# A head pair's order on five engines in hand, with its array visits, query casts and weight pieces moved, in a chunk-select attention with a routed expert layer

## The chip, the cores and the metric

The kernel runs on one core of one Trainium2 chip. The metric is the device time of one execution in microseconds (us), lower is better. The core has TensorE (PE; PEld is its weight load), VectorE (DVE), ScalarE (ACT), GpSimd (POOL), SyncE (SP), and 16 DMA engines that SP, ACT and POOL feed.

## The reference

Two stages follow each other. Attention: 4 batches, 8 heads, 768 positions, head size 64. Keys are cut into chunks of 32; for each query an upper bound of its score with any key of a chunk is formed, and the query attends, causally, to the 6 chunks of the highest bound:

```python
ub = np.sum(np.maximum(q[:, :, :, None, :] * k_min[:, :, None, :, :],
                       q[:, :, :, None, :] * k_max[:, :, None, :, :]), axis=-1)
ub = np.where(causal, ub, -1e9)
top_chunks = np.argsort(ub, axis=-1)[..., -top_k:]
...
attn = softmax of q @ k.T / 8 over the kept positions        # in words
x = (attn @ v) as 3072 tokens x 512
```

Then every token goes to the one expert of 8 with the highest logit `x @ w_gate`, and its output row is `gate * (relu(x @ w1[e]) @ w2[e])`, with w1 512x1024 and w2 1024x512 for each expert and gate the softmax probability of that expert.

## The kernel before, in words

**Tiling.** Attention runs over 16 head pairs `i` (4 in a batch; `hp = i % 4`). The two heads of a pair lie side by side in partitions. Scores are formed transposed (keys in partitions, queries in columns, queries in two halves of 384) in seven units `u`, 0 and 1 for the first query half, 2 to 6 for the second. A unit is one score tile in PSUM (two buffers, `ps_s`), an exp on ACT (L303), a causal `affine_select` on POOL for diagonal blocks (L307), a product with V on PE that collects in `po` (L320, `attend`), and an addition on DVE of the exponentials to an accumulator that gives the softmax sum (L332). Units 1 and 6 hold two key blocks, of 256 and 128 columns, each with an exp and an addition of its own. The chunk choice enters the scores as extra rows of the two operands: rows 64 and up of `KTE` name the chunk of a key, those of `QSB` hold which chunks a query does not take.

**Steps of a pair besides its units.** For pair `i+2`: K's two halves transposed on PE, their chunk maxima and minima on DVE (L207, L208) and scaled copies on ACT (L209, L210), in `k_half`; Q's halves transposed, copied on DVE and ACT (L224 to L227), and the query operand of head 0 cast on POOL (L226, kept back in `late` until a `flush`); sums and differences of maxima and minima (`kse`, L233 and L234). For pair `i+1`: the bound product (`ub`, L241), its choice of chunks on DVE (`select`, L249 to L262), and the mask's transposes (`mask`, L269) with two copies on ACT. For pair `i-1`: a product `ud` (L348, L353) that yields the softmax sums and the gate logits, its transposes `lgp` (L361), and the output rows `x0`, `x1` (L386, L388). Once a batch is complete its tokens are routed: `logits` (L398 to L422), `rank` (L432 to L448) and six scatters to HBM (L454). All small PSUM tiles share one pool of three buffers, `ps_m`.

**Array shapes.** The trace shows PE's matmuls as 128*128, 128*64 (L320, L241, L269) and 128*32 (`ud`).

**Order.** PE, POOL and SP follow the order of the code (`manual_schedule`); DVE and ACT are ordered by a scheduler, except in the first pair and from pair 15 on. The driver runs each pair in four groups g = 0 to 3: scores of units 2 and 3, then 4 and 5, then 6, then units 0 and 1 of pair `i+1`; in each, other steps stand between the scores and the attend products:

```python
groups = [(0, 1), (2, 3), (4, 5), (6,)]
spread = ((), (0,), (2, 4), (1,), (3, 5), (), (), ())
        wq += [4 * i + g for g in ((0, 1, 2) if i in (1, 3, 4, 8, 12) else (1, 2))]
```

`wq` sets in which group each of 32 weight pieces (512 KB, `load_w`, L169, issued by POOL) is fetched; pair 15 has none. `load` fetches K and Q of pair `i+3` in group 3 and V of pair `i+1` in group 0, issued by SP. `spread` sets where a batch's scatters go.

**The second stage.** A table of 28 tiles of 128 tokens of one expert is built in two parts (`table`, the first in pairs 13 and 14, L477 on). A tile's rows are gathered from HBM (L554, POOL), transposed by DMA (`x_in`, L566, SP), multiplied by w1 (`up`, L601), passed through ReLU (L604, ACT), transposed by DMA again (`hT`, L605, SP), multiplied by w2 (`down`, L612), scaled by the gate and scattered to the output (L620). Gathers 0 to 3 are issued at the start of pair 15, 4 to 7 in its third group; they use four buffers, freed by `x_in` and `meta`. `up` and `down` address the weights through a register.

Of the kernel before, what the change touches and what calls it, by code (L numbers as in the profile page):

```python
# [24 lines left out]
def kernel(  # L25
# [10 lines left out]
    nc = tc.nc  # L36
# [63 lines left out]
    KS = [buf.tile([128, 64], FP32, name=f"KS{i}") for i in range(2)]  # L100
    KD = [buf.tile([128, 64], FP32, name=f"KD{i}") for i in range(2)]
# [6 lines left out]
    def consts_first():  # L108
# [12 lines left out]
        nc.gpsimd.memset(KS[0][:], 0.0)  # L121
        nc.gpsimd.memset(KD[0][:], 0.0)
# [15 lines left out]
    def consts_last():  # L138
        nc.gpsimd.memset(KS[1][:], 0.0)
        nc.gpsimd.memset(KD[1][:], 0.0)  # L140
# [7 lines left out]
        nc.sync.dma_start(out=wgb[64:128, :, E:2 * E], in_=wg_v[64:128])  # L148
        iota(rev8[:], [[-1, E]], base=E)
# [11 lines left out]
    def load_w(s_):  # L161
# [7 lines left out]
        nc.gpsimd.dma_start(out=dst, in_=src.rearrange("(c p) f -> p c f", p=128))  # L169
# [24 lines left out]
    def prep_steps(i):  # L194
        s = st[i]
        kte, qsb, ks, kd = KTE[i % 2], QSB[i % 2], KS[i % 2], KD[i % 2]
        kmx = {}

        def k_half(hf):
# [3 lines left out]
            pt = ps_m.tile([128, 384], FP32, tag="m")  # L203
            for t in range(3):
                nc.tensor.transpose(pt[:, ts(t, 128)], s["k"][:, 3 * hf + t], ident_f[:])
            pk = pt[:].rearrange("p (c w) -> p c w", w=CH)
            nc.vector.tensor_reduce(s["kmx"][:, ts(hf, 12)], pk, AX.X, ALU.max)  # L207
            nc.vector.tensor_reduce(s["kmn"][:, ts(hf, 12)], pk, AX.X, ALU.min)  # L208
            nc.scalar.activation(kte[0:64, 0, ts(hf, 384)], pt[0:64, :], AF.Copy, bias=0.0, scale=0.125)  # L209
            nc.scalar.activation(kte[0:64, 1, ts(hf, 384)], pt[64:128, :], AF.Copy, bias=0.0, scale=0.125)  # L210

        def q_t(hf):
            pt = ps_m.tile([128, 384], FP32, tag="m")
            for t in range(3):
                nc.tensor.transpose(pt[:, ts(t, 128)], s["q"][:, 3 * hf + t], ident_f[:])
            s[f"qp{hf}"] = pt

        def q_e(hf):
            pt = s[f"qp{hf}"]
            if hf == 0:  # L220
                s["qT"] = work.tile([128, 2, 384], FP32, tag="qT", name="qT")
                s["qA"] = work.tile([128, 2, 384], FP32, tag="qA", name="qA")
            qT, qA = s["qT"], s["qA"]
            nc.vector.tensor_copy(out=qT[:, hf], in_=pt[:])  # L224
            nc.scalar.activation(qA[:, hf], pt[:], AF.Abs)
            late.append(lambda: nc.gpsimd.tensor_copy(out=qsb[0:64, 0, ts(hf, 384)], in_=qT[0:64, hf]))  # L226
            nc.scalar.activation(qsb[0:64, 1, ts(hf, 384)], pt[64:128, :], AF.Copy)  # L227

        def kse():
            for hd in range(2):  # L230
                r = slice(64 * hd, 64 * hd + 64)
                c = slice(32 * hd, 32 * hd + NCH)
                nc.vector.tensor_tensor(ks[r, c], s["kmx"][r, :], s["kmn"][r, :], ALU.add)  # L233
                nc.vector.tensor_tensor(kd[r, c], s["kmx"][r, :], s["kmn"][r, :], ALU.subtract)  # L234

        def ub():
            pu = ps_m.tile([128, 384], FP32, tag="m")
            for w_, nm in ((ks, "qT"), (kd, "qA")):
                x_ = s[nm][:].rearrange("p a c -> p (a c)")
                for h in range(2):  # L240
                    nc.tensor.matmul(pu[64 * h:64 * h + 64, 0:320], lhsT=w_[:], rhs=x_[:, ds(128 + 320 * h, 320)],  # L241
                                     start=(nm == "qT"), stop=(nm == "qA"), skip_group_check=True)
            s["ubT"] = work.tile([128, 384], FP32, tag="ud", name="ubT")
            nc.scalar.activation(s["ubT"][:, 0:320], pu[:, 0:320], AF.Copy)

        def select():
            pt = ps_m.tile([128, 3, 2, 2, 32], FP32, tag="m")
            for t in range(3):
                nc.tensor.transpose(pt[:, t], s["ubT"][:, ds(c0s[t], 128)], ident_f[:])  # L249
            ubm = work.tile([128, 3, 2, 2, NCH], FP32, tag="ubm")  # L250
# [623 lines left out]
```

## Time and profile before

| | |
|---|---|
| median of 3 runs | 359.88 us (358.68 to 360.48) |
| the profiled execution | 360.64 us |
| its span in the trace, granted clock | 358.6 us, 0.992 |
| busy share of the span: PE, DVE, ACT, POOL | 91, 66, 64, 50% |
| attention, up to the first `up` | 0 to 243.1 us |
| from one `lgp` (L361) to the next, pairs with no routing | 13.66 us |
| the same, pairs 5 and 9, which rank a batch | 15.51 us |
| weight pieces, issue to landing, median | 6.0 us |
| up and down of one token tile on PE, late in the second stage | 3.45 us |

A line of a timeline gives start and length in us, engine, line, operation, what is written and read, the number of instructions joined in it, and in brackets the idle time ahead of it with what ended it. A start is to be read against its neighbours: `L361` at 128.29 and at 141.95 delimit a pair. Busy shares are of the whole span; In the last third DVE is nearly idle and ACT half idle, so in the first two thirds they are far busier than the table says.

### The profile page before, as it was taken

How to read it: one execution, taken by the hardware profiler on the slowest of the kernel's cores; microseconds unless marked ns; L12 is line 12 of the kernel's file. 1: busy time of each engine (PE TensorE's matmuls, PEld its weight loads, DVE VectorE, ACT ScalarE, POOL GpSimd, SP SyncE). 2: the span in 40 equal slices, each digit the busy share in tenths (PEclk: the TensorE clock that was granted, in tenths of full speed). 3: DMA queues.
4: the chain of work that ended last, by engine and by line, in shares of the span. 5: the costliest groups of instructions: out<-in, count | busy, mean ns of one | idle time of the engine just before them, and what ended most of it. 6: DMA issues, size and time to landing. Idle time of an engine off the chain costs nothing. (4 is left out here: it accounts for less than half of the span.)

```text
span 358.6 us, 7585 instructions
## 1 busy us (share of the span) xinstructions
PE 326.9 (91%) x2312; PEld 171.5 (48%) x2312; DVE 235.0 (66%) x815; ACT 231.2 (64%) x398; POOL 180.4 (50%) x296
## 2 busy tenths in 40 slices
PE   6679999999899999999999988998799999999990
PEld 5535455455455465554554545443344344444430
DVE  5799889889999898999988999846460000000000
ACT  2497797797687897867977967642344444445440
POOL 3075425445474453466534547575577665653331
PEclk9999999999999999999999999999999999999996
DMA  8619998999957999937989973476999999998851
GB/s 153 112 26 194 210 220 139 215 167 215 207 127 151 182 176 195 202 100 178 200 134 212 187 148 113 73 135 116 165 211 233 221 237 197 203 186 201 157 126 48
DMA packets 138215, 59.83 MB, mean 167 GB/s; under 512 B 122811, under 2 KB 131005, under 8 KB 138176
## 3 DMA queue, kind: packets, MB, share of 16 engines
q1 hardware_dynamic: 119072, 29.52, 45.4%
q0 software_dynamic: 17536, 29.42, 42.0%
q10 hardware_dynamic: 1568, 0.39, 0.6%
q8 instruction: 21, 0.34, 0.4%
q14 instruction: 18, 0.15, 0.2%
HBM read 56.14 MB, written 10.51 MB: 186 GB/s over the span
## 5 line engine op out<-in xcount | busy, mean ns | idle before, releaser
L332 DVE TENSOR_TENSOR Pa<-Pa,Pr 128x768 f32<-128x768 f32 (+2 forms) x112 | 81.6, 729 | 1.1
L307 POOL TENSOR_SCALAR_AFFINE_SELECT Pr<-Pr 128x256 f32<-128x256 f32 x80 | 33.5, 437 | 67.3 <-ACT Pr L303 66.1
L303 ACT ACTIVATE Pr<-ps 128x768 f32<-128x768 f32 (+2 forms) x112 | 65.0, 630 | 3.2 <-PE ps L298 2.9
L612 PE MATMUL py<-w_all,hT 128*128 x224 | 52.7, 379 | 2.7 <-DMA hT<-h__3653 1.9
L298 PE MATMUL ps<-QSB,KTE 128*128 128x384 bf16 (+2 forms) x288 | 50.4, 292 | 1.2 <-DVE QSB L711 0.2
L620 POOL DMA_INDIRECT out_dram<-y,ti_all x28 | 27.8, 993 | 30.2 <-ACT y L619 26.3
L298 PEld LDWEIGHTS <-KTE 128*128 128x128 bf16 x288 | 24.1, 97 | 27.3 <-issue 21.2
L612 PEld LDWEIGHTS <-hT 128*128 128x128 bf16 x224 | 21.8, 98 | 29.5 <-DMA hT<-h__3653 2.3
L619 ACT ACTIVATE y<-py,gt_all 128x512 f32<-128x512 f32 x27 | 18.6, 687 | 20.8 <-PE py L612 18.4
L454 POOL DMA_INDIRECT xs_dram<-xrow,sli x24 | 26.9, 1121 | 7.7 <-issue 5.0
L356 ACT ACTIVATE ud<-pu 128x384 f32<-128x384 f32 x16 | 7.9, 492 | 32.8 <-PE pu L353 30.7
L303 ACT ACTIVATE Pa<-ps 128x768 f32<-128x768 f32 x32 | 26.0, 812 | 3.8 <-PE ps L298 3.2
L601 PE MATMUL ph<-w_all,KTE 128*128 x120 | 28.4, 379 | 0.0
L169 POOL DMA_DIRECT2D w_all<-in_moe_w_dram x32 | 24.3, 760 | 0.0
L307 POOL TENSOR_SCALAR_AFFINE_SELECT Pa<-Pa 128x256 f32<-128x256 f32 x16 | 6.4, 398 | 35.3 <-ACT Pa L303 35.3
L601 PE MATMUL ph<-w_all,QSB 128*128 x96 | 22.7, 379 | 0.3 <-issue 0.3
L575 DVE TENSOR_TENSOR ti_all<-xgqA,inv_i 128x1 int32<-128x1 int32 x9 | 1.4, 159 | 29.6 <-DMA xgqA<-xs_dram,grow 29.6
L554 POOL DMA_INDIRECT xgqA<-xs_dram,grow x14 | 14.6, 1046 | 10.2 <-issue 3.3
L554 POOL DMA_INDIRECT xgqT<-xs_dram,grow x14 | 14.5, 1033 | 8.7 <-DVE gt_all L577 4.9
L325 DVE COPY ot<-po 128x384 f32<-128x384 f32 x32 | 17.7, 553 | 1.6 <-PE po L320 0.9
L575 DVE TENSOR_TENSOR ti_all<-xgqT,inv_i 128x1 int32<-128x1 int32 x8 | 1.3, 159 | 26.5 <-DMA xgqT<-xs_dram,grow 26.5
L226 POOL CAST QSB<-qT 64x384 bf16<-64x384 f32 x30 | 16.3, 551 | 4.1 <-DVE qT L224 2.8
(311 smaller groups left out, 665.0 us busy)
## 6 DMA issues: line engine op xcount, KB each, us to landing
w_all<-in_moe_w_dram POOLq DMA_DIRECT2D x32, 512.0 KB, 6.0
out_dram<-y,ti_all POOLq DMA_INDIRECT x28, 3.6
t__122<-in_k_dram SPq DMA_DIRECT2D x2, 192.0 KB, 3.5
t__125<-in_q_dram ACTq DMA_DIRECT2D x2, 192.0 KB, 4.0
t__128<-in_v_dram SPq DMA_DIRECT2D x2, 192.0 KB
t__196<-in_k_dram SPq DMA_DIRECT2D x2, 192.0 KB, 3.1
t__206<-in_q_dram SPq DMA_DIRECT2D x2, 192.0 KB, 3.8
t__209<-in_v_dram SPq DMA_DIRECT2D x2, 192.0 KB
```

Source lines behind the costliest of these rows:

```text
L169: nc.gpsimd.dma_start(out=dst, in_=src.rearrange("(c p) f -> p c f", p=128))
L298: nc.tensor.matmul(pv[:, hd, :], lhsT=kte[:, hd, ts(kb, 128)], rhs=qsb[:, hd, ds(qb * 384 + 384 - w, w)], start=True, stop=True, skip_grou ...
L303: nc.scalar.activation(P[:, :, ds(c0, w)], pv, AF.Exp)
L307: nc.gpsimd.affine_select(out=pd, in_=pd, pattern=[[0, 2], [1, 128]], compare_op=ALU.is_ge, fill=0.0, base=0, channel_multiplier=-1)
L325: nc.vector.tensor_copy(out=ot[:], in_=po[:])
L332: nc.vector.tensor_tensor(acc[:, :, 384 - w:384], acc[:, :, 384 - w:384], P[:, :, ds(c0, w)], ALU.add)
L454: d = nc.gpsimd.indirect_dma_start(out=xs_dram[:], out_offset=bass.IndirectOffsetOnAxis(ap=sli[:, u:u + 1], axis=0), in_=bst[b][f"xrow{u % ...
L554: d = nc.gpsimd.indirect_dma_start(out=xg_bufs[j % XB].bitcast(I32), out_offset=None, in_=xs_dram[:], in_offset=bass.IndirectOffsetOnAxis( ...
L601: nc.tensor.matmul(ph[:, fh, :], lhsT=xT[:, c, :], rhs=w_all[:, ds(wo + (c * F + fh * 512), 512)], start=(c == 0), stop=(c == NDC - 1), sk ...
L612: nc.tensor.matmul(py[:], lhsT=hT[:, c, :], rhs=w_all[:, ds(wo + (W1W + c * DM), DM)], start=(c == 0), stop=(c == NFC - 1))
L619: nc.scalar.activation(y[:], py[:], AF.Copy, bias=0.0, scale=fs[j]["gt"])
L620: d = nc.gpsimd.indirect_dma_start(out=out[:], out_offset=bass.IndirectOffsetOnAxis(ap=fs[j]["ti"], axis=0), in_=y[:], in_offset=None, bou ...
```

## The change

- `KS` and `KD` become one tile `KSD`; `kse` has three DVE operations for four, one of them a product with a constant block mask `bm`.
- The constants of routing and table leave `consts_last` for `consts_route`, called in pair 2, group 2.
- w2's pieces are loaded with `(p c) f` rows, a partition's four rows of w2 adjacent in HBM; ReLU writes h in the matching order, reading PSUM in strides of four.
- All steps are cut into a PE part (`_mm`), a DVE part (`_v`) and an ACT part (`_a`), and DVE and ACT follow the order of the code throughout.
- A unit's columns lie at the same place in each head's half of the score tile, so units 1 and 6 have one exp. Unit 6 is scored in halves of 64 keys (`split`), eight matmuls for four.
- The driver has another order: unit 6's scores move from group 2 to the end of group 1, `ud` behind them, and the mask behind `ud`. K's first half goes from group 2 to group 1, its ACT copies ahead of its DVE reductions. The additions of units 5 and 6 go to the next pair's group 0. The query casts on POOL (`flush(late)`) go from group 0 to group 1, ahead of unit 6's affine selects.
- Logits of a batch go from group 3 of the pair with hp = 0 to group 0 of the next, and are whole there; rank, exp and gates follow in its group 1, the scatters in other groups.
- Weight pieces go by `npiece`: one at the start of group 0, the others in group 1; pair 15 has three, issued after gathers 0 to 3 and ahead of gathers 4 to 7.

The diff, cut to its core:

```diff
-        nc.gpsimd.dma_start(out=dst, in_=src.rearrange("(c p) f -> p c f", p=128))
+        nc.gpsimd.dma_start(out=dst, in_=src.rearrange("(c p) f -> p c f" if n < 2 else "(p c) f -> p c f", p=128))
...
+        def kse():
+            kt2 = work.tile([128, 2, NCH], FP32, tag="top8", name="kt2")
+            nc.vector.tensor_tensor(kt2[:, 0], s["kmx"][:], s["kmn"][:], ALU.add)
+            nc.vector.tensor_tensor(kt2[:, 1], s["kmx"][:], s["kmn"][:], ALU.subtract)
+            nc.vector.tensor_tensor(ksd[:, :, :, 0:NCH], kt2[:].unsqueeze(2).to_broadcast([128, 2, 2, NCH]),
+                                    bm[:].unsqueeze(1).to_broadcast([128, 2, 2, NCH]), ALU.mult)
...
+        n = 64 if split else 128
+        for kb, w, c0 in parts:
+            for hd in range(2):
+                for h in range(128 // n):
+                    nc.tensor.matmul(ps[ds(h * n, n), hd, ds(c0, w)], lhsT=kte[:, hd, ds(kb * 128 + h * n, n)],
+                                     rhs=qsb[:, hd, ds(qb * 384 + 384 - w, w)],
+                                     start=True, stop=True, skip_group_check=True)
...
-        for pv, (kb, w, c0) in zip(pvs, parts):
-            nc.scalar.activation(P[:, :, ds(c0, w)], pv, AF.Exp)
+        nc.scalar.activation(P[:], ps[:, :, 0:384], AF.Exp)
...
-            nc.scalar.activation(h_[:], ph[:], AF.Relu)
+            nc.scalar.activation(h_[:].rearrange("q a (c p) -> q a c p", c=4),
+                                 ph[:].rearrange("q a (p c) -> q a c p", c=4), AF.Relu)
...
+    spread = ((), (), (0, 2, 4), (), (1, 3), (5,), (), ())
+    npiece = [2, 2, 2, 2, 2, 1, 2, 2, 2, 1, 2, 2, 2, 2, 3, 3]
...
-    with tc.manual_schedule(engines={PE, POOL, SP}):
+    with tc.manual_schedule(engines={PE, POOL, SP, DVE, ACT}):
...
                 if g == 0:
+                    pieces(i, 1)
+                    for u in (2, 3):
+                        scores(i, u)
+                        exps(i, u)
+                    run(rout, i - 2, "x_mm", 1)
+                    run(rout, i - 2, "x_v", 1)
+                    if i > 0:
+                        if n < NP:
+                            add(i - 1, 5)
+                        add(i - 1, 6)
+                    av(i, 0)
+                    av(i, 1)
+                    o_ev(i, 0)
+                    if router:
+                        logits()
+                    add(i, 1)
+                    run(prep, n, "ub")
+                    run(prep, n, "ub_a")
+                    if 0 < i < NP - 1:
+                        load(n, "v")
                 elif g == 1:
+                    for u in (4, 5):
+                        scores(i, u)
+                        exps(i, u)
+                    run(prep, n, "sel_mm")
+                    if i > 0:
+                        run(prep, m, "k_mm", 0)
+                        run(prep, m, "k_a", 0)
+                    if router:
+                        rank_mm()
+                    run(prep, n, "sel_v")
+                    if router:
+                        expo()
+                        rank_v()
+                        gates()
+                    if i > 0:
+                        run(prep, m, "k_v", 0)
+                    av(i, 2)
+                    av(i, 3)
+                    add(i, 3)
+                    flush(late)
+                    pieces(i, 3 if i >= 14 else 1)
+                    scores(i, 6, True)
+                    exps(i, 6)
+                    run(rout, i - 1, "ud")
+                    run(rout, i - 1, "ud_a")
                 elif g == 2:
...
+                    run(prep, n, "mask")
+                    run(prep, n, "mask_a")
...
+                    av(i, 4)
+                    av(i, 5)
+                    add(i, 4)
+                    if m >= NP:
+                        add(i, 5)
+                    flush(sums_)
                 else:
+                    run(rout, i - 1, "lgp_mm")
+                    run(rout, i - 1, "x_mm", 0)
+                    if n < NP:
+                        for u in (0, 1):
+                            scores(n, u)
+                            exps(n, u)
+                    run(rout, i - 1, "lgp_v")
+                    run(rout, i - 1, "x_v", 0)
+                    run(prep, m, "k_mm", 1)
+                    run(prep, m, "k_v", 1)
+                    run(prep, m, "k_a", 1)
+                    for hf in range(2):
+                        run(prep, m, "q_mm", hf)
+                        run(prep, m, "q_v", hf)
+                        run(prep, m, "q_a", hf)
                     if i + 3 < NP:
                         load(i + 3, "k", "q")
+                    av(i, 6)
+                    o_ev(i, 1)
+                    run(prep, m, "kse")
+                    if hp == 0 and b > 0:
+                        flush(sums_)
...
+                if 4 * i + g == 10:
+                    consts_route()
```

In pair 15 the pieces of its group 1 thus stand in POOL's order behind the query casts and ahead of unit 6's two affine selects, which gathers 4 to 7 follow. `run` does nothing for a pair outside 0 to 15; `pieces(i, n)` issues up to n of the pair's remaining pieces. `consts_route` holds what `consts_last` had from L149 on.

## The prediction

> **What bounds the kernel now.** I read the table by stretches of 30 us first: it says whether one engine fills every stage.
>
> ```profile
> 30.00:60.00 30.00, 29.36 (x233) 16.02 (x228) 27.05 (x81) 25.54 (x48) 11.76 (x25) 1.00 1.06 186
> 120.00:150.00 30.00, 29.77 (x238) 16.12 (x234) 27.88 (x87) 25.35 (x48) 12.93 (x27) 1.00 1.10 184
> 240.00:270.00 30.00, 26.15 (x150) 12.44 (x151) 16.04 (x79) 10.12 (x13) 18.39 (x23) 1.00 0.90 158
> 270.00:300.00 30.00, 29.13 (x135) 13.11 (x134) 2.02 (x18) 14.20 (x18) 19.52 (x20) 1.00 1.06 221
> ```
>
> Columns: PE, PEld, DVE, ACT, POOL busy, clock, DMA share. Attention (0 to about 243) has PE at 98%, but DVE at 92% and ACT at 84% close behind: three engines in a ring. The MoE tiles (from about 255) are PE alone. The hole is at 240 to 270.
>
> Then the timelines of PE, ACT and DVE in one head pair (logits transpose to logits transpose, L361, 128.29 to 141.95 = 13.66 us; pairs that also route take 15.51):
>
> ```profile
> 135.50 1.06 PE L298 MATMUL ps<-QSB,KTE 128*128 128x384 bf16 x4
> 141.95 0.55 PE L361 MATMUL pt<-ident_f,ud 128*128 128x128 f32 x3
> 145.44 0.82 PE L298 MATMUL ps<-QSB,KTE 128*128 128x384 bf16 x4
> ```
> ```profile
> 145.13 0.48 ACT L209 ACTIVATE KTE<-pt 64x384 bf16<-64x384 f32 x1 [0.21 <-DVE kmn L208]
> ...
> 147.15 0.81 ACT L303 ACTIVATE Pa<-ps 128x768 f32<-128x768 f32 x1
> 147.86 0.48 ACT L225 ACTIVATE qA<-pt 128x384 f32<-128x384 f32 x1
> 148.37 0.49 ACT L227 ACTIVATE QSB<-pt 64x384 bf16<-64x384 f32 x1
> 148.88 0.81 ACT L303 ACTIVATE Pr<-ps 128x768 f32<-128x768 f32 x1
> ```
>
> Two score units cost 0.82 us free (145.44) and 1.06 at 135.50: unit 5 there waits until ACT's exp of unit 3 frees a PSUM buffer. That closes a ring: logits transpose 141.95, DVE's reductions of K, ACT's K copies at 145.13, four 0.49 copies, exp 2, exp 3 ending 149.69: 7.74 us; from unit 5's start to the next L361 PE needs 5.9 us more. 7.74 + 5.9 = 13.66. PE's own slots sum to 13.25, so 0.41 a pair is waiting.
>
> The end of attention, from the timelines of POOL, SP and PE:
>
> ```profile
> 242.14 1.02 POOL L554 DMA_INDIRECT xgqT<-xs_dram,grow  x1 [1.13 <-DVE gt_all L577]
> 243.73 1.01 POOL L554 DMA_INDIRECT xgqT<-xs_dram,grow  x1 [0.56 <-DVE Pa L332]
> ```
> ```profile
> 245.14 3.85 SPq L566 DMA_TRANSPOSE QSB<-xgqT  x2
> 249.08 1.26 SPq L605 DMA_TRANSPOSE hT<-h__3653  x1
> ```
> ```profile
> 255.04 1.89 PE L612 MATMUL py<-w_all,hT 128*128 x8 [1.86 <-DMA hT<-h__3653]
> ```
>
> The first down product stands on the transpose of h, which stands on SP behind the transposes of tiles 4 and 5, and these behind gathers 4 and 5. After it PE has no hole; whatever moves it moves the end.
>
> **What the skill says.** "TensorEngine Tiling (Array Packing)", Key Properties: changing the tiling mode drains TensorE. The trace agrees: gaps at a change of mode are 0.05 to 0.13 us over the spacing within a mode. "PSUM — Partial Sum Buffer", PSUM bank collisions: ACT and DVE must not touch one bank and quadrant together, so readers are ordered; the trace has it as ACT's K copy waiting for DVE kmn above. "DMA: Bandwidth & Descriptors", Two DMAs through the same engine are not ordered: descriptors within one queue of a DMA engine start in order; SWDGE vs HWDGE in the same page gives POOL's issues one queue. No place in the trace of before has gathers issued behind pieces that still wait, so it neither shows nor denies it.
>
> **Part by part**, from L361 to L361, then the end.
>
> *PE order.* Nine mode changes become eight, about -0.15 by the gaps above; unit 6's scores in 64-column halves double four matmuls to eight (+0.06 to +0.11) and end in a further change (+0.10). Sum 0; bounds -0.15 to +0.15 a pair. So PE's floor stays 13.25.
>
> *The ring.* Merged exps (592 + 390 = 982 ns become one 816) save ACT 0.3 a pair, but units 1 and 6 lie outside the ring, so 0. K's first half goes to the second group, ACT copy ahead of DVE's reductions: off the ring. L361 to the reductions of K's second half stays about 1.98, +1.01 for them, four or so 0.51 copies, two exps: 7.72; unit 5 to L361 by the slots 5.86. 13.58, -0.08 a pair, times nine plain pairs: -0.7. What is hidden by PE's wait is at most 0.41 a pair, the gain if the ring opened.
>
> *DVE.* The K sums fall from four operations to three (-0.3, one took 0.48 beside the POOL cast). Delayed adds now follow each other on one accumulator. In DVE's timeline an unrelated operation follows a 768-column add after 0.86 us (138.52 to 139.38), an add on the same accumulator after 2.01 - 0.95 = 1.06 (the two at 242.75), so four such cost +0.8. DVE has 13.66 - 1.05 idle = 12.61 now; 12.61 - 0.3 + 0.8 = 13.1 of 13.58: it still fits, 0.5 spare. If it didn't, the rest would go onto the ring.
>
> *Constants.* The route constants leave the first pair's DVE queue (about -0.6 before the first selection) and come in pair 2, some 12 small DVE operations, 1.5 us, ahead of the reductions of the ring: 0.5 is spare, so +1.0. Net +0.4; bounds -0.6 (all hidden) to +0.9.
>
> *Routing pairs.* Now whole chains on DVE by hand. Before's last batch shows a chain uninterleaved:
>
> ```profile
> 254.63 0.21 DVE L398 TENSOR_TENSOR lg<-lg 128x48 f32<-128x48 f32 x1 [1.14 <-POOL lg L378]
> 254.88 0.20 DVE L400 TENSOR_REDUCE rmax<-lg 128x6 f32<-128x48 f32 x1
> ...
> 255.84 0.21 DVE L411 TENSOR_TENSOR oh<-cand,m 128x48 bf16<-128x48 f32 x1
> ...
> 258.98 0.21 DVE L441 TENSOR_TENSOR rk<-pr,base_e 128x48 f32<-128x48 f32 x1 [2.10 <-PE pr L438]
> ...
> 259.78 0.15 DVE L448 TENSOR_TENSOR base_e<-base_e,pr 128x8 f32<-128x8 f32 x1
> ```
>
> 1.4 for logits, 0.95 for the ranks, 0.7 for the gates. Queued behind them on DVE is K's first reduction; PSUM has three buffers in ps_m, and with the rank tile among them the mask's transposes get the buffer of that K half, free only after the reduction. On PE the mask has two attend groups and L361 queued behind it. Its wait puts L361 to L361 at 16.75 against 15.51 (+1.24), and the pair after at 13.58 against 13.92 (-0.34): +0.9 for each of pairs 5 and 9. Pair 13 the same +1.24, pair 14, with the early table as a chain, 16.1 against 15.55 (+0.55), pair 15 10.7 against 11.15 (-0.45): +1.35. Bounds: 0, if the buffer is free in time, to +5 in all.
>
> *POOL's casts and scatters.* The two query casts (0.55 each) come ahead of unit 6's affine selects instead of a group later; those selects get up to 1.1 later, and the attend product that needs them comes a group (over 3 us) later: 0, if that cover were gone +1.1. Six scatters (about 1.1 each) move by a group or two within half-idle POOL; ahead of affine selects one could cost 1.1, the next product is 2 us off: 0.
>
> *Weight pieces.* In pairs 0 to 14 their place is off PE's path (POOL is half idle, an issue is 0.76): 0; without that cover 0.76 an affine select. The 4 KB packets of w2 shorten q0's time, which nobody waits for: 0. But pair 15 had none and gets three: one behind gathers 0 to 3, two ahead of the last unit's affine selects and gathers 4 to 7. SP isn't passed; POOL's three issues put the selects 2.3 us later (the last attend product waits, +0.5, mostly hidden by later waits). A piece of 512 KB took about 3 us of all engines; three take 9, beginning where gather 4's issue was nearly due. In ring order gather 4 moves from L361 + 13.9 to + 20.2, the transpose of tile 5 ends at + 23.9 and h's is issued at + 24.0 instead of + 19.1; down(0) at + 29.2 against 25.05: +4.1. up(0) reads the weights by a register and waits for the last w1 piece, near + 15 instead of + 13.1, but PE has a 1.2 us hole right behind it and the wait for h: 0 beside the 4.1. Bounds 0 (gathers overtake, or the pieces start early) to +5.
>
> *ReLU* reads PSUM in strides of four for w2's row order. No row shows that: 1.02 contiguous; from 0 (below nothing excluded, more work can't be quicker) to double. ACT is half idle in the MoE stage and h's transpose has about 3 us of slack: 0, at most +1.
>
> **Sum** against the profiled execution, 360.64 us (span 358.6): -0.7 + 0.4 + 1.8 + 1.35 + 4.1 + 0.2 (what of the select shift shows) = +7.15; 367.8 for it. The median of the runs shown is 359.88, 0.76 lower: 367.0.
>
> **Rivals.** (a) The tail is not delayed: gathers 4 to 7 interleave with the pieces. For: nothing in before proves ring order. Against: one queue. Then 359.9 + 2.85 = 362.7, a little more with the selects. (b) Faster: the hand order takes the waiting out, since K's first half no longer comes between unit 6 and the mask and ACT has 0.3 less: plain and following pairs run at PE's floor, 11 x -0.41 = -4.5, the routing stalls and the tail's delay at nothing: 355.4. It decides from the point where exp 3 ends 0.33 us earlier after L361 (7.4 instead of 7.72). Against: the chain of copies is the same. (c) Half of each: the ring opens, the tail delay stays: 359.9 - 4.5 + 4.3 = 359.7. That w2's rows don't change is excluded by the diff; that they bring time is against the DMA share, on which no PE row waits.
>
> **Numbers.** 0.5% (1.8 us) is about what a measurement of this kernel can tell from no change. Forecast 0.45 (363.5 to 371 on its own), (a) 0.20, (b) 0.22, (c) 0.13. Range 356 to 371: down to just above (b), up to the upper bounds of routing or tail. Faster 0.22, same 0.13, slower 0.65.
>
> **What would show it.** L361 intervals of 13.6 plain and 16.7 in pairs 5 and 9, mask transposes waiting for DVE's K reduction; unit 5 still waiting for exp 3; gathers 4 and 5 landing after the last piece; down(0) some 4 us later from pair 14's L361 and waiting for h. Wrong if plain intervals fall to 13.3, or down(0) keeps 25 us.

## The result and the profile after

The changed kernel takes 381.79 us (median of 4 runs, 379.71 to 384.13) against 360.12: a ratio of 1.0612 [1.0531, 1.0692], 21.7 us slower (medians are over all runs of a kernel; the ratios leave out those that took over 1.5% more than its fastest). The forecast was 367.0, slower by 7, with a range up to 371. The profiled execution took 379.71 us, its span is 378.0 and its mean clock 0.960; before it was 360.64, 358.6 and 0.992.

Where the 19.4 us between the spans lie, in us (`lgp` is L361 before and L386 after; `down` is L612 and L654):

| stretch | before | after | difference |
|---|---|---|---|
| start to the first `lgp` (pair 1) | 44.23 | 50.00 | +5.8 |
| first `lgp` to that of pair 14 | 185.76 | 192.11 | +6.35 |
| from there to the first `down` product | 25.05 | 37.42 | +12.4 |
| to the issue of the last output scatter | 95.2 | 93.8 | -1.4 |
| from that issue to the end of the span | 8.3 | 4.6 | -3.7 |

The -1.4 is no more than what this stretch differs from profile to profile: with the order of before it took 97.2 and 97.0 us in two others, on another chip of about the same speed (experiment 9).

The stretches of 30 us of the changed kernel, columns as in the prediction (PE, PEld, DVE, ACT, POOL busy, clock, DMA share):

```profile
30.00:60.00 30.00, 25.91 (x194) 14.90 (x196) 22.93 (x63) 22.36 (x39) 8.22 (x18) 0.94 0.89 174
120.00:150.00 30.00, 29.41 (x260) 16.63 (x256) 28.55 (x91) 23.95 (x41) 14.89 (x29) 1.00 0.88 168
240.00:270.00 30.00, 16.80 (x122) 8.36 (x124) 12.76 (x31) 8.25 (x11) 16.01 (x21) 0.88 0.76 153
270.00:300.00 30.00, 28.94 (x144) 12.91 (x146) 12.83 (x69) 11.92 (x15) 17.19 (x20) 0.90 0.76 154
```

In the middle (120 to 150) PE is as full as before. In two stretches it isn't: 30 to 60, with 25.9 for 29.4, and 240 to 270, with 16.8 for 26.2. In both, and from 270 to 300, the clock is below 1.00, which it was nowhere there before. The page's row of the clock, in 40 slices of 9.45 us and in tenths of full speed, and its row for POOL's queue (packets, MB, share of the 16 engines' time):

```profile
PEclk9898999899999999999999998998589999999998
...
q0 software_dynamic: 11392, 29.42, 37.9%
```

**The intervals from `lgp` to `lgp`.** Forecast and measured, difference to before summed over the intervals:

| intervals that end in | forecast | measured |
|---|---|---|
| the plain and following pairs 2, 4, 6 to 8, 10 to 12 and routing pairs 5, 9, 13 | +2.3 | -0.2 |
| pair 3 (constants in pair 2) | +1.0 | +2.86 |
| pair 14 (first part of the table) | +0.55 | +3.69 |

Pair 14 follows a routing pair, as pairs 6 and 10 do, which lost 1.2 and 0.7 without any table; so not all of its 3.69 need be the table's.

A plain pair takes 13.39 to 13.52 (forecast 13.58, before 13.66), 13.81 where it is the second after a routing one. PE's timeline in one of them; the two score units of group 1 still wait for an exp (1.06 for 0.82 free), as in the ring of before:

```profile
144.48 1.06 PE L311 MATMUL ps<-QSB,KTE 128*128 128x384 bf16 x4
...
150.81 0.55 PE L386 MATMUL pl<-ident_f,ud 128*128 128x128 f32 x3
```

A routing pair takes 15.07, not 16.75, and the loss is carried into the next: 15.10 and 14.58. DVE's timeline at the end of pair 5's interval and the start of pair 6's shows it:

```profile
105.67 0.20 DVE L481 TENSOR_TENSOR rk<-pr,base_e 128x48 f32<-128x48 f32 x1
...
107.45 0.55 DVE L212 TENSOR_REDUCE kmx<-pk 128x12 f32<-128x384 f32 x1
...
111.31 0.55 DVE L212 TENSOR_REDUCE kmx<-pk 128x12 f32<-128x384 f32 x1
```

The chain of ranks and gates (105.67 to 107.45) holds K's first reduction, as forecast. But the mask on PE waited only 0.67, for ACT's copy of `ud`. What came late was the next item on DVE's list, the reduction of K's second half at 111.31, after the additions of two units; PE waited 0.79 for it there.

**PE's large waits**, all in its own timeline. The lengths of what follows them are to be read too: eight attend products of 256 columns take 0.87 at 139.95, and 1.47 at 67.83; seven of 384 columns take 1.46 at 149.43, and 2.76 at 34.62. That is TensorE at half its clock: the trace's record of the clock has it at one half from 16.8 to 20.2, 33.8 to 37.2, 68.0 to 71.4, 228.4 to 231.8, 262.5 to 276.2 and at the very end.

```profile
33.48 0.56 PE L207 MATMUL pk<-ident_f,t__363 128*128 128x128 f32 x3 [4.04 <-DMA t__363<-in_k_dram]
...
34.62 2.76 PE L342 MATMUL po<-Pr,t__125 128*64 128x384 f32 x7
...
66.94 0.97 PE L234 MATMUL pq<-ident_f,t__750 128*128 128x128 f32 x6 [1.68 <-issue]
67.83 1.47 PE L342 MATMUL po<-Pr,t__600 128*64 128x256 f32 x8
...
227.51 0.97 PE L234 MATMUL pq<-ident_f,t__3077 128*128 128x128 f32 x6 [2.77 <-issue]
...
240.37 0.47 PE L287 MATMUL pm<-ident_b,nsel 128*64 128x128 bf16 x5 [1.86 <-DVE nsel L280]
```

What stood in front of them, from the timelines of POOL and SP (`POOL`, `SPq`) and of DVE:

```profile
25.66 0.90 POOL L172 DMA_DIRECT2D w_all<-in_moe_w_dram  x1
26.22 1.12 SPq L193 DMA_DIRECT2D t__363<-in_k_dram  x2
...
65.06 0.29 DVE L159 TENSOR_SCALAR U<-colf,iota_p 128x128 bf16<-128x128 f32 x1 [1.12 <-POOL colf L105]
...
224.74 0.16 DVE L521 TENSOR_TENSOR cnt<-base_e,ebase 128x8 f32<-128x8 f32 x1
...
236.26 0.24 DVE L550 TENSOR_TENSOR gt<-ge,coef 128x88 f32<-128x88 f32 x1
```

At 33.48 PE waits for the K of pair 2, whose load SP issued at 26.22, right behind pair 0's first weight piece (POOL, 25.66). Before, the load was issued at 24.72 and the piece at 26.97, and PE waited 0.51. At 66.94 PE waits while DVE makes the constants (from 65.06, after 1.12 of waiting for POOL's `iota`); behind them stand `lgp_v`, with whose end, at 66.8, PE goes on, and K's reduction. At 227.51 and 240.37 the first and third part of the table stand on DVE (224.74 to 226.8, 236.26 to 238.3) ahead of `lgp_v` and ahead of the choice of chunks.

The half clock at 16.8 to 20.2 lies in the prologue. The profile of before has none there, but experiment 2 and the first of experiment 9, which have before's prologue, do; their first `lgp` comes at 45.86 and 46.04, against 44.23 to 45.46 in the five profiles of that prologue without it. So some 1.5 of the start's 5.8 can befall the kernel before as well.

**The tail.** SP's transpose of tile 2, then all engines from 264 on, in order of time:

```profile
253.07 1.19 SPq L606 DMA_TRANSPOSE KTE<-xgqA  x1
...
264.67 1.00 POOL L594 DMA_INDIRECT xgqA<-xs_dram,grow  x1 [5.74 <-DMA KTE<-xgqA]
265.68 2.50 SPq L606 DMA_TRANSPOSE QSB<-xgqT  x2
267.15 0.99 POOL L594 DMA_INDIRECT xgqA<-xs_dram,grow  x1 [1.48 <-DMA QSB<-xgqA]
268.16 0.86 POOL L407 TENSOR_TENSOR lg<-lg,lgt 128x96 f32<-128x96 f32 x2
268.27 1.26 SPq L647 DMA_TRANSPOSE hT<-h__3680  x1
269.06 0.42 DVE L396 TENSOR_TENSOR lgt<-pl,rec 128x96 f32<-128x96 f32 x2 [12.25 <-POOL lg L407]
...
269.63 1.46 PE L370 MATMUL pu<-Pa,dcol 128*32 128x384 f32 x2 [10.32 <-DVE lgt L396]
...
274.06 2.92 PE L642 MATMUL ph<-w_all,KTE 128*128 x8
...
279.53 1.89 PE L654 MATMUL py<-w_all,hT 128*128 x7
```

Read it backwards. `ud` of the last pair (269.63) waited 10.32 us for DVE, DVE for POOL's sums of the gate logits (L407), and these stood in POOL's order behind gathers 6 and 7 (L594), which waited for their buffers. The buffers are freed by the transposes of tiles 2 and 3. Tile 2's was issued at 253.07 and released gather 6 at 264.67, 11.6 us later; before, such a transpose took 2.8 to 6.1 us from issue to landing (median 4.2 from 240 to 275). Beside it ran the last three weight pieces (packets from 253.7 to 264.5, so 10.8 us where the forecast had 9). The transpose of h, on which the forecast stood, was issued 26.2 us after pair 14's `lgp` (forecast 24.0, before 19.1), and the first `down` no longer waits for it: it comes later still, in PE's order behind `ud` and two `up`s, the first at half clock (2.92 for 1.89).

### The profile page after: what moved, and what is told of

It is laid out like the page before. It is cut to its first block, busy times and chain, and to the rows that moved or that the text cites. A ratio compares the mean times of both kernels' runs of the same rounds, so it can differ in the third digit from the quotient of the medians.

```text
span 378.0 us, 7552 instructions
## 1 busy us (share of the span) xinstructions
PE 333.2 (88%) x2366; PEld 180.3 (48%) x2376; DVE 238.3 (63%) x799; ACT 229.2 (61%) x366; POOL 184.3 (49%) x297
## 3 DMA queue, kind: packets, MB, share of 16 engines
q0 software_dynamic: 11392, 29.42, 37.9%
## 5 line engine op out<-in xcount | busy, mean ns | idle before, releaser
L329 POOL TENSOR_SCALAR_AFFINE_SELECT Pr<-Pr 128x256 f32<-128x256 f32 x80 | 38.2, 496 | 84.6 <-ACT Pr L325 84.5
L325 ACT ACTIVATE Pr<-ps 128x768 f32<-128x768 f32 x80 | 63.3, 816 | 13.6 <-PE ps L311 8.3
L311 PE MATMUL ps<-QSB,KTE 128*128 128x384 bf16 (+4 forms) x352 | 51.6, 290 | 1.3 <-ACT Pr L325 0.4
L654 PE MATMUL py<-w_all,hT 128*128 x219 | 52.2, 379 | 0.6 <-DMA hT<-h__3991 0.3
L311 PEld LDWEIGHTS <-KTE 128*128 128x128 bf16 (+1 forms) x352 | 27.0, 104 | 28.8 <-issue 23.2
L218 ACT ACTIVATE KTE<-pk 64x384 bf16<-64x384 f32 x60 | 29.2, 487 | 13.5 <-DVE kmn L213 13.1
L325 ACT ACTIVATE Pa<-ps 128x768 f32<-128x768 f32 x32 | 26.0, 812 | 15.2 <-PE ps L311 14.8
L654 PEld LDWEIGHTS <-hT 128*128 128x128 bf16 x224 | 21.8, 98 | 26.7 <-DMA hT<-h__3991 0.7
L494 POOL DMA_INDIRECT xs_dram<-xrow,sli x24 | 24.6, 1023 | 9.0 <-issue 5.7
L293 ACT ACTIVATE QSB<-pm 24x640 bf16<-24x640 bf16 x30 | 20.8, 693 | 8.8 <-PE pm L287 8.3
L370 PE MATMUL pu<-Pa,dcol 128*32 128x384 f32 x128 | 15.7, 520 | 11.2 <-DVE lgt L396 10.3
L212 DVE TENSOR_REDUCE kmx<-pk 128x12 f32<-128x384 f32 x32 | 17.6, 549 | 11.4 <-PE pk L207 11.4
L172 POOL DMA_DIRECT2D w_all<-in_moe_w_dram x32 | 21.3, 667 | 0.0
L594 POOL DMA_INDIRECT xgqA<-xs_dram,grow x14 | 14.4, 1032 | 14.0 <-DMA KTE<-xgqA 5.7
L594 POOL DMA_INDIRECT xgqT<-xs_dram,grow x14 | 15.0, 1073 | 10.4 <-issue 4.3
```

Source lines behind the costliest of these rows:

```text
L218: nc.scalar.activation(kte[0:64, hd, ts(hf, 384)], pt[64 * hd:64 * hd + 64, :], AF.Copy, bias=0.0, scale=0.125)
L293: nc.scalar.activation(qsb[64:64 + NCH, hd, 128:S], s["pm"][32 * hd:32 * hd + NCH, 128:S], AF.Copy)
L311: nc.tensor.matmul(ps[ds(h * n, n), hd, ds(c0, w)], lhsT=kte[:, hd, ds(kb * 128 + h * n, n)], rhs=qsb[:, hd, ds(qb * 384 + 384 - w, w)], s ...
L325: nc.scalar.activation(P[:], ps[:, :, 0:384], AF.Exp)
L329: nc.gpsimd.affine_select(out=pd, in_=pd, pattern=[[0, 2], [1, 128]], compare_op=ALU.is_ge, fill=0.0, base=0, channel_multiplier=-1)
L494: d = nc.gpsimd.indirect_dma_start(out=xs_dram[:], out_offset=bass.IndirectOffsetOnAxis(ap=sli[:, u:u + 1], axis=0), in_=bst[b][f"xrow{u % ...
```

## The experiments

The runs fell on chips on which the kernel before took 359.5 to 367.6 us, so ratios and times of stretches are compared. Theory: four displacements (a piece ahead of a load, the constants, the table's parts, the logit sums and pieces of the tail) and the half clock that follows their waits. Rivals: the ring order of the queue alone in the tail, or the clock as a cause of its own, or the split of unit 6. Stretches differ between profiles of one kernel too: with before's order and no piece in pair 15, that from pair 14's `lgp` to the first `down` took 21.7 to 25.1 us in six profiles.

**1. The tail without pieces** (the changed kernel, pair 15 has none).

```diff
-    npiece = [2, 2, 2, 2, 2, 1, 2, 2, 2, 1, 2, 2, 2, 2, 3, 3]
+    npiece = [2, 2, 2, 2, 2, 2, 2, 2, 2, 2, 2, 2, 3, 3, 2, 0]
...
-                    pieces(i, 3 if i >= 14 else 1)
+                    pieces(i, 3)
```

> The changed kernel with the three weight pieces of pair 15 moved into pairs 5, 9, 12 and 13, so that pair 15 issues none. Theory (the pieces fill the DMA engines just when the transposes of token tiles 2 and 3 and gathers 4 to 7 need them, and POOL's waiting gathers hold up the logit sums behind them): the first down product comes 25 to 27 us after pair 14's logits transpose instead of 37.4, time about 370 (11 to 12 us less than 381.8). The prediction's own chain (only gathers 4 and 5 late): 4 us less, about 378. Rival (the tail is late because TensorE's clock dropped, whatever the pieces do): 2 us less or nothing.

Measured: 380.71, ratio 1.0376 [1.0284, 1.0468]; from pair 14's `lgp` to the first `down` 28.18 (37.41 and 36.90 in experiments 4 and 5, on the same chip, with the tail as it was). So the pieces are needed for 9.2 of the 12.4. What is left still has the wait of `ud` for DVE's logits, now 4.69: the sums behind gathers.

**2. The kernel before, with pieces where the change has them** (w2 still in before's rows).

```diff
                     x_in(j)
+                load_w(29)
...
+                    if i == NP - 1:
+                        load_w(30)
+                        load_w(31)
                     scores(i, 6)
...
-                    if wq[n] == 4 * i + g:
+                    if wq[n] == 4 * i + g and n < 29:
```

> The kernel before with its last three weight pieces moved into pair 15, one behind gathers 0 to 3 and two ahead of the last unit's scores and gathers 4 to 7, nothing else. Theory: the same jam, +9 to +12 us, about 370; the prediction's chain: +4, about 364; if the jam needs the changed order of the other steps: within 1 us of 360.

Measured: 375.87, 1.0297 [1.0197, 1.0398], so about 11 us (7 to 15); the stretch 30.68, so +5.6 against the profile of before, and +7.6 against a second one, on a chip as slow as this (23.04). PE's timeline:

```profile
262.60 3.55 PE L612 MATMUL py<-w_all,hT 128*128 x8 [6.23 <-DMA hT<-h__3653]
```

The first `down` waits for h: this is the forecast's chain, alone, since in this kernel the sums of pair 14 stand ahead of the gathers. It costs more than the 4.1 that the forecast gave it. The stretch stays under the 9 to 12 us of the theory; the time as a whole doesn't exclude them.

**3. The logit sums ahead of the gathers** (the changed kernel, `flush(sums_)` of pair 15 at the start of its group 0).

```diff
                     pieces(i, 1)
+                    if i == NP - 1:
+                        flush(sums_)
```

> The changed kernel with the pending logit sums of POOL flushed at the start of pair 15, as the kernel before had them, instead of behind gathers 4 to 7; the pieces stay in pair 15. Theory (the jam of the DMA engines costs about 5.6 us by itself, as it did in the kernel before with these pieces; the sums behind four waiting gathers make it 12): DVE's logit products no longer wait 12 us for POOL, the first down product 30 to 32 us after pair 14's logits transpose instead of 37.4, time 6 us less than the changed kernel. Rival (the sums' place is harmless and the gathers alone set it): at most 1 us less.

Measured: 376.12, 1.0486 [1.0393, 1.058], against 1.0641 [1.0557, 1.0724] for the unchanged changed kernel on that chip, 4.9 us less; the stretch 31.15 for 38.11 there. PE's timeline:

```profile
272.59 1.01 PE L654 MATMUL py<-w_all,hT 128*128 x2 [4.07 <-DMA hT<-h__3680]
```

The wait of `ud` is gone and the wait for h is back. The tail is two chains on top of each other: the forecast's, and a longer one through POOL's order that hid it. The forecast's alone is still 6.7 us over the 24.5 of the mended kernel below, and again more than 4.1.

**4. K ahead of the first piece** (pair 0's pieces both in group 1).

```diff
-                    pieces(i, 1)
+                    pieces(i, int(i > 0))
...
-                    pieces(i, 3 if i >= 14 else 1)
+                    pieces(i, 3 if i >= 14 or i == 0 else 1)
```

> The changed kernel with the first weight piece of pair 0 in its group 1 instead of group 0, so that pair 2's K and Q loads come first in time. Theory (the piece holds the K load back, PE waits 4.0 us for it and then runs 3.4 us at half clock): 5 to 6 us less, about 376, first logits transpose near 44.5 instead of 50.0. Rival (the load is late for another reason, such as its own late issue): at most 1 us less.

Measured: the wait for K 1.37 for 4.04, the first `lgp` at 46.53 for 50.00; 385.82, 1.0536 [1.0447, 1.0625], a ratio that does not stand clear of the changed kernel's. So 3.5 of the start's 5.8 go with this one issue: 2.7 of waiting, and 0.8 that fits the half clock behind it, which is gone too; both profiles have the one in the prologue. Experiment 1, on the same chip and with the changed kernel's start, waited 4.62 for K, lacks the half clock in the prologue, and has its first `lgp` at 48.30; with some 1.5 for that half clock the two comparisons agree.

**5. The constants at the prologue's end** (`consts_route()` moved there whole).

> The changed kernel with the routing constants back in the prologue, ahead of the second pair's steps. Theory (in pair 2 they hold DVE behind POOL's iotas, PE stands 1.7 us and falls to half clock for 3.4 us, 2.9 us in all; in the prologue DVE has room): 2 to 3 us less, about 379, the interval of pair 3's logits transpose 13.4 to 13.7 instead of 16.5. The prediction's sum had 0.4 for it.

Measured: 392.05, 1.0729 [1.0622, 1.0836], no gain. The interval that ends in pair 3 fell to 13.39 as expected, but PE waited 8.31 us up to 28.94 in the prologue, because DVE waited:

```profile
25.82 0.28 DVE L159 TENSOR_SCALAR U<-colf,iota_p 128x128 bf16<-128x128 f32 x1 [7.63 <-POOL colf L105]
```

In this hand order DVE stopped at the first operation that needed POOL's `iota`, and POOL reached it late. The first `lgp` came at 52.86. So in both places the constants cost what their operands made DVE wait.

**6. Is it the clock?** Spare matmuls on `ones_b` ahead of two K transposes, so that PE isn't idle in the waits there (60 in pair 0, 28 in pair 2), beside the changed kernel unaltered.

> The changed kernel with idle TensorE time filled in two places by matmuls of ones whose output is overwritten: 60 ahead of K's first half in pair 0 (where PE waits 4.0 us for the load) and 28 ahead of K's second half in pair 2 (where it waits 1.7 us behind the routing constants). The waits stay. Theory (each wait costs itself and then about 1.6 us because the clock is halved for 3.4 us): 2.5 to 3.3 us less than the changed kernel, no half-clock stretch behind either wait. Rival (the half clock is hidden by the waits of the other engines): within 0.5 us of the changed kernel, although the clock stays up.

> The changed kernel itself, for runs on the same chip as the following ones: 1.05 to 1.07 of the kernel before.

Measured: 381.91 and 381.06, 1.065 [1.0564, 1.0737] and 1.0641 [1.0557, 1.0724]. The expected 2.5 to 3.3 us do not come. The half clock is gone behind both waits, but stands at 16.7 to 20.1 (as in the first profile) and 238.6 to 242.0 (and in the tail, as in both). The interval that ends in pair 3 is 15.31 with the spare matmuls and 15.30 without, as that run had no half clock there, though the same wait of 1.68 us; in the first profile, which had it, 16.53. So half a clock cost about 1.2 us there, where it met a full PE; its places change from run to run, and behind waits of this length it comes in some runs and not in others. This run can't say what the clock is worth in all.

**7. All mended**: 1, 3 and 4 together, `iota`s in the prologue with DVE's part in pair 0, the table's three parts moved one, two and two groups later (and a few small temporaries of both in other buffers).

```diff
-                if 4 * i + g == 10:
+                if 4 * i + g == 1:
                     consts_route()
-                if 4 * i + g in (4 * NP - 10, 4 * NP - 9, 4 * NP - 8):
+                if 4 * i + g in (4 * NP - 9, 4 * NP - 7, 4 * NP - 6):
```

> The changed kernel with the suspected places mended together: no piece in pair 15, the first pieces of pair 0 in group 1, the logit sums ahead of gathers 4 to 7, the routing constants made by POOL in the prologue and by DVE in pair 0 behind group 1, the three parts of the early table behind groups (13,3), (14,1) and (14,2) instead of (13,2), (13,3) and (14,0). Theory (these places hold nearly all of the loss, and the reordered steady pairs none): pair 14's logits transpose at 230 to 233 us, the first down product 25 to 26 us later, the whole within 1.2% of the kernel before, either way. Rival (the hand order itself costs, by routing pairs and dependent additions): 2.5% or more above it.

> The mended kernel once more, beside the kernel before with w2's rows alone. If the hand order still costs something that w2's rows repay: 3 to 5 us slower than the kernel before with these rows, 0.997 to 1.003 of the kernel before.

Measured: 358.66, 0.9991 [0.9963, 1.002], and on another chip 366.62, 0.9963 [0.994, 0.9987]. First `lgp` 45.17, to pair 14's 185.5, to the first `down` 24.46; the interval that ends in pair 3 is 13.38. In the profile the losses of the start, the constants and the tail are gone, and the time is within 0.4% of that of the kernel before. Of the table's a part is left: the interval that ends in pair 14 is 15.19, the next 14.16 for 11.15 before. PE's timeline there:

```profile
236.76 1.17 PE L344 MATMUL po<-Pa,t__3388 128*64 128x384 f32 x4 [2.44 <-issue]
```

**8. The table a slot later still, and without the split** (both from 7; the second also scores unit 6 in four matmuls).

```diff
-                if 4 * i + g in (4 * NP - 9, 4 * NP - 7, 4 * NP - 6):
+                if 4 * i + g in (4 * NP - 9, 4 * NP - 7, 4 * NP - 5):
...
-                    scores(i, 6, True)
+                    scores(i, 6)
```

> The mended kernel with the last part of the early table behind pair 14's group 3 instead of group 2, so that the copy that frees the output buffer of PSUM goes ahead of it on DVE. Theory: pair 15's first attend product no longer waits 2.4 us and PE keeps its clock; the interval between the logits transposes of pairs 14 and 15 falls from 14.2 to 11 to 12 us while gathers 0 to 3 start 0.5 us later; 2 to 3 us less than the mended kernel, 0.99 to 0.994 of the kernel before. Rival (the later gathers take it back): the same as the mended kernel.

> The previous kernel with unit 6 scored in four matmuls of the full array instead of eight of half its columns. Theory (the change of mode that is saved is worth what the split costs): plain pairs within 0.1 us of 13.5, time within 1.6 us of the previous kernel. Rival (the three visits are a gain of their own): plain pairs at 13.8 or more, 3 us or more slower.

Measured: 366.99, 1.0025 [1.0003, 1.0048], and 366.93, 0.9968 [0.9939, 0.9998]. The later slot gained nothing that shows: the interval that ends in pair 15 is 13.78 for 14.16, where 11 to 12 were expected. Without the split plain pairs take 13.5 to 13.6 for 13.4 to 13.5, so there the split is worth 0.1 us a pair. But from the first `lgp` to pair 14's the kernel without it took 185.5 us against 186.6, and the ratios lean the same way: over the whole the split isn't shown to gain. As a cause of 21.7 us it is out.

**9. w2's rows alone, in parts.** The kernel before with w2 in 8 KB rows and the ReLU to match; the transfers only; the ReLU only; the changed kernel with the old rows; and the kernel before again. With the transfers or the ReLU alone, h meets w2's rows in another order: the result changes, the amount of work doesn't.

```diff
-        nc.gpsimd.dma_start(out=dst, in_=src.rearrange("(c p) f -> p c f", p=128))
+        nc.gpsimd.dma_start(out=dst, in_=src.rearrange("(c p) f -> p c f" if n < 2 else "(p c) f -> p c f", p=128))
```

> The kernel before with w2's pieces in 8 KB rows and ReLU reading in strides of four, nothing else. Theory (no PE row waits for the pieces, and ACT has room for a slower ReLU): within 0.4% of the kernel before, either way; ReLU near the 1.02 us it takes now. Rival (shorter piece transfers let the other loads through, or ease the transposes of the second stage): 1% or more faster.

> The kernel before with w2's rows alone, once more, beside a profile of the kernel before on the same chip. If the 1.1% of its first run is the rows' doing: 0.985 to 0.994 again, with the difference in the end of attention or in waits of the second stage. If it was that chip's slow DMA: 0.996 to 1.004 where the kernel before runs at 360.

> The kernel before with only the transfers of w2 in 8 KB rows; ReLU leaves h in the old order, so that the second product pairs h with the wrong rows of w2 (a changed computation of the same size). Theory (the transfers make the 1.0 to 1.1% that w2's rows measured twice): 0.985 to 0.994 of the kernel before. Rival (the order in which ReLU reads makes it, or only both together): 0.997 to 1.003.

> The kernel before with only ReLU's strided reading, w2 loaded as before, so that again h meets the wrong rows of w2. Theory (transfers make it): 0.997 to 1.003 of the kernel before, ReLU at 1.02 us. Rival: 0.985 to 0.994.

> The changed kernel with w2's rows as before, everything else changed. Theory (the rows shorten the jam in pair 15, two of whose three pieces are w2's, and the second stage): 3 to 6 us slower than the changed kernel, the first down product later than 38 us behind pair 14's logits transpose. Rival (no part of the rows' gain shows in the changed kernel): within 1.5 us of it.

> The kernel before itself, for a profile on the same chip as the following runs: 1.000 of the kernel before, within 0.4%.

| kernel | us | ratio | last scatter to the end |
|---|---|---|---|
| before, new rows and ReLU | 362.38 | 0.9893 [0.985, 0.9937] | 4.3 |
| the same, another chip | 364.17 | 0.9897 [0.9866, 0.9927] | 4.3 |
| before, transfers only | 356.60 | 0.9894 [0.9854, 0.9934] | 4.4 |
| before, ReLU only | 360.54 | 0.9998 [0.9973, 1.0023] | 8.3 |
| after, old rows | 391.88 | 1.0673 [1.0624, 1.0723] | 8.6 |
| before again | 367.21 | 0.9986 [0.9946, 1.0025] | 8.3 |

The first of these was expected to change nothing and gained about 1%, on two chips; the transfers alone gained as much on a third, the ReLU alone nothing. The gain thus comes with the transfers. The one stretch that is shorter in every profile, and by as much, is the one behind the last scatter; a single pair of profiles need not show it in the whole (362.7 with the rows and ReLU, 363.0 for before again, on one chip), as other stretches differ by 1 to 2 us from run to run. The last scatter of the kernel before, of the changed one, and of before with the new transfers, each followed by no more work on any engine (spans 358.6, 378.0, 354.9):

```profile
350.27 0.98 POOL L620 DMA_INDIRECT out_dram<-y,ti_all  x1 [1.22 <-DVE y L617]
```
```profile
373.36 0.97 POOL L662 DMA_INDIRECT out_dram<-y,ti_all  x1 [1.06 <-DVE y L659]
```
```profile
350.50 0.98 POOL L620 DMA_INDIRECT out_dram<-y,ti_all  x1 [1.21 <-DVE y L617]
```

In all 19 profiles the end comes 8.3 to 8.6 us after this issue where POOL's queue had 17536 packets, and 4.3 to 5.1 where it had 11392. Most of it is one DRAIN, an instruction of POOL's sequencer that stands on the line that calls the kernel (L869, L968). The two lines give, before and after, the shortest, the median and the longest of three DRAINs in ns:

```profile
L869 POOLq DRAIN  x3: 51/103/5215, 352.5 to 358.3; - x3
```
```profile
L968 POOLq DRAIN  x3: 51/103/2095, 375.1 to 377.7; - x3
```

It takes 5.21 us in each of the five profiles with 17536 packets and 2.07 to 2.56 in the 14 with 11392; another such instruction ahead of it, INC_SWDGE_SEM, takes 1.46 in before and 0.60 in after. In before it begins at 352.54, just as the last packet of POOL's queue ends (352.55), so it doesn't stand for packets of that queue still under way. Why it takes longer there isn't shown; that it is work counted in packets is a guess, from two counts. The changed kernel without the new rows is 0.3 to 0.6% slower than with them, which the intervals do not separate, and its first `down` came earlier (35.7 us behind pair 14's `lgp`), where later than 38 had been expected.

**The version that beats both** is the kernel before with w2's rows alone: 0.989. On the chip where both ran, all of it mended (366.62) is 2.4 us slower than that (364.17).

## Why the prediction was wrong

The sign and the place of the largest loss were right; the size was off by 14.8 us. The step that failed most is the sum for pair 15's weight pieces, 12.4 for 4.1; beside it, four terms put at or near nothing measured 3.5 (pieces of pair 0), 1.6 to 2.9 (constants), up to 3.7 (table) and -3.7 (w2's rows). By its own steps:

- *PE order, ring, DVE* (plain pairs -0.7): right. The six plain intervals sum to -0.73, forecast for nine; they range from -0.27 to +0.14 where -0.08 was forecast for each, so that the sums agree is in part luck. PE's place in the ring is unchanged, and rivals (b) and (c), which needed it to open, fell.
- *Routing pairs* (+1.8 and +1.24): too much. They measured +0.97 for pairs 5 and 9 with those that follow, and -0.44 for pair 13. DVE's chain did hold K's first reduction; that the mask would wait for that buffer was wrong, and the slip went to K's second half.
- *Weight pieces, "pair 15 +4.1"*: the ring order was right (experiments 2 and 3), rival (a) fell. The term was mis-sized, 12.4 for 4.1, for two reasons. One step wasn't costed: POOL's logit sums moved past the gathers. The forecast listed the casts and scatters that POOL's queue was given in another place, and left these out. And the pieces alone cost more than 4.1, in experiment 2 5.6 to 7.6; they ran 10.8 us for 9. Moving the sums takes the tail from 38.1 to 31.2, and doing without the pieces as well, in the mended kernel, to 24.5. Taken the other way round the pieces are worth more (37.4 to 28.2) and the sums less (to 24.5), since each chain hides a part of the other.
- *Weight pieces, "pairs 0 to 14: 0"*: failed. "Off PE's path" was argued from POOL's idle time and not from the 16 engines behind it; pair 0's first piece went ahead of the K load that PE needs next: 3.5 us. The start had no term but the -0.6 of the constants: "PE at 98%" was read for 0 to 243 us, but holds from 30 on; the page of before has PE at 60 to 79% in its first three slices, 27 us.
- *Constants* (+0.4): failed. 1.6 to 2.9 in the interval that ends in pair 3, by their count of operations and by a wait for POOL that was in no row.
- *The table in pair 14* (+0.55): failed, +3.69, of which the pair's place behind a routing one may be a part. Two of the table's three parts, placed by hand, hold DVE for about 2 us each just ahead of the step that PE needs; before, a scheduler placed them. Its cost as a chain was read from the last batch's routing, not from the table's own operations.
- *The clock*: missing from the forecast. All waits were costed at their length.
- *w2's rows* ("nobody waits for q0: 0"): failed in the other direction, -3.7 at the end. *ReLU* 0 (1.02 us as before) and *the split* 0: right within what the runs can tell.

"TensorE: Matmul & The Clock Gate", Part 1, of the Trainium skill says that the clock falls to half after at least one idle window of about 3.4 us and comes back after about 3.4 us of work, with windows that run freely. The length of the half-clock stretches here agrees (33.8 to 37.2, 68.0 to 71.4, 228.4 to 231.8), and so does their moving from run to run. But behind waits of 1.7 to 2.8 us (1.68 at 66.94, 2.77 at 227.51) they came as well, though not in every run; the measurement decides. "DMA: Bandwidth & Descriptors", Queues, rings and completion order, says that each DMA engine takes turns among its queues, packet by packet. The packets of the trace agree in part. From 257.1 us on those of the transposes of tiles 2 and 3, on SP's queue, ran among the pieces' on POOL's, 1024 in 8.7 us; before, 512 took 0.6 to 2.2. But the first of them ran only 4.0 us after tile 2's issue at 253.07 (before, 1.2 after), and from 253.9 to 257.1 only packets of the pieces ran; turns among queues don't explain that, and no run here does.

Open: why POOL's DRAIN at the program's end takes longer with the old rows; how much of the 21.7 us is clock; and why the mended order doesn't keep the whole gain of w2's rows. Its profile in experiment 7 has the shorter close (span 355.7), and nowhere a stretch over 0.9 us longer than in the profile of before, but its median is 2.4 us above that of the rows alone. Its profile can't settle it: on the chip where both ran, the profiled execution of the mended order (363.13) is the fastest of its 22.

## What to carry to other kernels

When an order is written by hand, list for every moved call all instructions that it issues, on each engine, and ask of each what it now stands in front of and what its operand waits for: three of the four losses here were small operations (two sums, a dozen constants, a table's part) ahead of a critical one in a queue. A transfer that nobody waits for still needs a place: put it behind the load that PE needs next, not by the idle time of the engine that issues it. Try the parts of a bundle alone; here one that was costed at nothing was the only gain that shows in the whole time.

## What the hardware showed that was not expected

- TensorE ran at half clock for 3.4 us at a time after waits of only 1.7 to 2.8 us, in some runs and not in others; once that cost 1.2 us in a pair (16.53 against 15.30 with the same wait).
- The program's end comes 8.3 to 8.6 us after the last scatter's issue with 17536 packets on POOL's queue and 4.3 to 5.1 us with 11392, over 19 profiles. Most of the difference is one DRAIN of POOL, 5.21 us against 2.07 to 2.56.
- A DMA transpose that lands in 2.8 to 6.1 us took 11.6 beside three weight pieces of 512 KB; its first packet ran 4.0 us after its issue (1.2 before).
